# Attention into a mixture of experts on one core: rows written straight into their expert's list

## The chip, the cores and the metric

One core of a Trainium2 chip runs the whole program. The metric is device microseconds per execution; lower is better. Besides the times there is one profiled execution, whose trace gives the start and duration of every instruction and DMA, and who released whom.

## The reference

There are four batches of 3648 tokens with 256 channels. Attention runs over channels: q and k are normalized along the tokens, the 256 x 256 scores of a batch are summed over its tokens, and x = v @ softmax(scores). Then each token of x goes to one of 16 experts (4 groups of 4), and its result is weighted by two softmax values:

```python
qn = q / (np.linalg.norm(q, axis=1, keepdims=True) + 1e-06)
kn = k / (np.linalg.norm(k, axis=1, keepdims=True) + 1e-06)
a = softmax(kn.transpose(0, 2, 1) @ qn / tau)         # 4 x 256 x 256
x = (v @ a).reshape(14592, 256)
g = argmax(x @ w_group); e = argmax(x @ w_expert[g])  # one expert a token
h = np.maximum(x[tok] @ w1[g, e], 0.0)                # 256 -> 1024
out[tok] = (g_w * e_w)[:, None] * (h @ w2[g, e])      # 1024 -> 256
```

All is float32. The kernel gets near that by splitting each operand into a high and a low part and multiplying three times (high x high, high x low, low x high).

## The kernel before

**Scores.** 32 steps load a tile of q and k each (GPB = 8 tiles a batch: seven of 4 columns of 128 tokens, and a short one), split it and multiply. When a batch's scores are complete, a softmax follows.

**The x stage** runs 10 steps later, one tile u of v a step: SP loads it (`x_load`, line 264, tile `vr`), PE transposes it (`x_tr`, line 276, `vtr`), PE multiplies (`x_mm`, line 294, `xmm`), and ACT copies the result (line 297) into one of three buffers `xs`: 256 words of x and 20 router logits a token. ACT then issues the DMA that writes x to a DRAM table in token order (`x_scratch`, line 304).

**Routing.** `routing(b, j0, j1)` runs on DVE over a range of a batch's columns. It finds each token's expert, its place in that expert's list (`si`) and its weight, kept as pairs (token, weight) in `pr`. RANGES says how batches are cut. `scatter` issues on POOL one indirect DMA a column (line 387): 128 pairs of 8 bytes, to the places `si` of a table `slot_list` in DRAM. After each indirect DMA POOL fills a dummy tile (`pause`, line 125). 116 columns make 116 scatters; the first 78 (`PRE`: batches 0 and 1 and 20 columns of batch 2) are enough for the first four items.

**Items.** The expert work is 28 items of up to 512 tokens of one expert (and some small pieces, `q`, of 4 x 32). `tables_pre` picks items 0 to 3 from the counts over PRE; `tables_rest` picks the others once every token has a place. For an item, SP loads the list (`fetch_ids`, line 513, `slt`) and the expert's two weight matrices (`fetch_w`, line 508, three buffers `wraw`, 1 MB each); POOL gathers the rows (`fetch_x`, four gathers of 128 rows, line 519, `xg`); PE transposes, ACT and DVE split the rows (`xth`, `xtl`, lines 569 and 570) and the weights (`wh` on ACT, line 544; `wl` on DVE, line 545). An item has 8 steps f: `ffn1` (line 670, `hmm`), relu and split (`hh` on ACT, line 674; `hl` on DVE, line 675), and two steps later `ffn2` (line 686, `yacc`). At the end `put` weights the rows and scatters them to the output on POOL (line 696).

**Order.** SP and POOL run in written order; SP's queue holds loads of v, of lists and of weights alike, and an entry that waits holds up those behind it. In the expert stage a scheduler orders PE, ACT and DVE; their order is then fixed. ACT splits item i+1's weights between the `hh` of item i.

Of the kernel before, what the change touches and what calls it, by code (L numbers as in the profile page):

```python
# [11 lines left out]
I32 = mybir.dt.int32  # L12
# [17 lines left out]
NE = C + NL  # L30
BIG = 512
# [11 lines left out]
RANGES = [[(0, 16), (16, NJ)], [(0, 16), (16, NJ)], [(0, 16), (16, 20), (20, NJ)], [(0, NJ)]]  # L43
# [3 lines left out]
LOADS = 3  # L47
SPLIT = 3
# [6 lines left out]
def attention_moe(ctx: ExitStack, tc, q, k, v, tau, w_group, w_expert, w1, w2, out):  # L55
# [6 lines left out]
    xd = nc.dram_tensor("x_scratch", (N, C), F32, kind="Internal").ap()  # L62
    sl = nc.dram_tensor("slot_list", (NSLOT, 2), I32, kind="Internal").ap()
# [6 lines left out]
    ps = ctx.enter_context(tc.tile_pool(name="ps", bufs=2, space=PSUM))  # L70

# [35 lines left out]
    prs = {}  # L107
    for b in range(B):
        for j0, j1 in RANGES[b]:
            prs[b, j0] = t = cp.tile([P, j1 - j0, 2], I32, name=f"pr{b}_{j0}")  # L110
            n = min(j1, J) - j0
            POOL.iota(t[:, :n, 0], pattern=[[1, n]], base=b * NT + j0, channel_multiplier=J)
            if j1 == NJ:
                POOL.iota(t[:, n:n + 1, 0], pattern=[[0, 1]], base=b * NT + J * P, channel_multiplier=1)
    xgs = []
    for i in range(3):
        t = cp.tile([P, 4, C], F32, name=f"xg{i}")
        POOL.memset(t, 0.0)
        xgs.append(t)

    pad = cp.tile([P, 256], F32, name="pad")
# [8 lines left out]
    def fill_slots():  # L130
        n = NSLOT // P
        slz = spool.tile([P, n // 2, 2], I32, tag="slz", name="slz", bufs=1)
        POOL.memset(slz[:, :, 0:1], NOID)
        POOL.memset(slz[:, :, 1:2], 0)
        for h in range(2):
            SP.dma_start(sl[h * NSLOT // 2:(h + 1) * NSLOT // 2, :].rearrange("(p n) w -> p n w", p=P), slz)
# [144 lines left out]
    def x_mm(u, mid=None):  # L281
# [6 lines left out]
        xs = tp.tile([P, GJ, NE], F32, tag="xs", name="xs", bufs=3)  # L288
# [19 lines left out]
    scatters, pend, now = [], [], [0]  # L308
# [4 lines left out]
    def routing(b, j0=0, j1=NJ):  # L313
        nj = j1 - j0
        L = st[b]["L"][:, j0:j1, :]
        pr = prs[b, j0]

        def wide(nm, n, *shape):
            return rp.tile([P, NJ * n], F32, name=nm)[:, 0:nj * n]
# [48 lines left out]
        si = rp.tile([P, NJ], I32, name="si", bufs=4)[:, 0:nj]  # L368
# [27 lines left out]
    def table(items, cnt, start, stride, name):  # L396

        inc = rp.tile([1, E], F32, tag="tinc", name="tinc")
        DVE.tensor_tensor_scan(inc, onesf[0:1, 0:E], cnt, 0.0, ALU.mult, ALU.add)
        ge = rp.tile([1, items, E], F32, tag="tge", name="tge")  # L400
        ii = iof[0:1, 0:items]
        ib = lambda a: a.unsqueeze(2).broadcast_to([1, items, E])
        eb = lambda a: a.unsqueeze(1).broadcast_to([1, items, E])
        DVE.tensor_tensor(ge, ib(ii), eb(inc), ALU.is_ge)
        ex = rp.tile([1, items], F32, tag="tex", name="tex")
        DVE.tensor_reduce(ex, ge, AX.X, ALU.add)
        DVE.tensor_tensor(ge, ge, eb(inc), ALU.mult)
# [9 lines left out]
        nv = rp.tile([1, items], F32, tag="tnv", name="tnv")  # L417
        DVE.tensor_scalar(nv, ex, float(E), None, ALU.is_lt)
        DVE.tensor_scalar(st_, st_, float(-DUMMY), None, ALU.add)
        DVE.tensor_tensor(st_, st_, nv, ALU.mult)  # L420
        tb = rp.tile([1, items, 2], I32, name="tb_" + name)
        DVE.tensor_scalar(tb[:, :, 0], ex, float(E - 1), None, ALU.min)
        DVE.tensor_scalar(tb[:, :, 1], st_, float(DUMMY), None, ALU.add)
        return tb

    r16 = lambda nm: rp.tile([1, E], F32, name=nm)

    def shifted(x, sh, nm):
        i_ = rp.tile([1, E], I32, tag="shi", name="shi")
# [8 lines left out]
    def tables_pre():  # L438
        cnt = carry[0:1, :]
# [619 lines left out]
```

## Time and profile before

| | |
|---|---|
| median of 3 runs | 1002.72 us (1001.12 to 1002.72) |
| the profiled execution's own time | 1002.05 us |
| its span, first to last instruction | 1000.3 us |
| mean granted TensorE clock | 0.982 |
| busy: PE, DVE, POOL, ACT | 945.1, 563.2, 515.3, 474.0 us |
| moved by DMA | 202.17 MB |

The span lies 1.75 us below the profiled time, and that lies 0.67 us below the median. PE is busy for 94% of the span, so the first question is where its other 55 us lie and what it waited for there. PEclk is the share of TensorE's full clock that was granted in a stretch. An instruction marked SPq is the issue of a DMA by SP, not its transfer. In a timeline the brackets give the engine's idle time ahead of an instruction and what ended it.

### The profile page before, as it was taken

Reading aid. Unit: us, or ns where it says so; the run is one execution under the profiler, and the core shown is the slowest. Engines: PE = TensorE matmul, PEld = TensorE weight load, DVE = VectorE, ACT = ScalarE, POOL = GpSimd, SP = SyncE. Lnnn points to the kernel's source line nnn. Section 1 sums busy time; section 2 is a strip of 40 time slices with the busy share of each in tenths; the row PEclk is TensorE's granted clock in tenths of the full one; section 3 lists DMA queues with packets and bytes.
Section 4 is the critical chain, followed back from the end, with each engine's and each line's share of the span. In section 5 each row is a group of like instructions: output and inputs, shape, how many; then the busy total and the mean of one; then the engine's idle time right before and its main releaser. Section 6 shows DMA issues by size and latency. Waiting matters only on the chain.

```text
span 1000.3 us, 18385 instructions
## 1 busy us (share of the span) xinstructions
PE 945.1 (94%) x6428; PEld 831.4 (83%) x6428; DVE 563.2 (56%) x961; ACT 474.0 (47%) x763; POOL 515.3 (52%) x729
## 2 busy tenths in 40 slices
PE   7999999978899399999999999999999999999995
PEld 6899989867789298888888888888888888888885
DVE  6988988774798154444444444454445444544421
ACT  6777767445644134443444444444444444444421
POOL 2001989885868854445444544455444544454322
PEclk9999999989999799999999999999999999999998
DMA  8898788358720546666666666556655665565520
GB/s 300 322 373 271 243 253 264 110 179 272 233 86 1 180 140 211 212 211 216 212 211 208 210 218 206 198 202 215 201 201 203 209 209 194 198 223 198 195 74 25
DMA packets 125685, 202.17 MB, mean 202 GB/s; under 512 B 18946, under 2 KB 87562, under 8 KB 125584
## 3 DMA queue, kind: packets, MB, share of 16 engines
q1 hardware_dynamic: 93952, 155.92, 47.0%
q0 software_dynamic: 15040, 30.03, 8.5%
q10 hardware_dynamic: 16592, 14.97, 4.5%
q8 instruction: 52, 0.85, 0.4%
q14 instruction: 49, 0.40, 0.1%
HBM read 169.49 MB, written 32.43 MB: 202 GB/s over the span
## 4 chain that ended last, share of the span: by engine, by line
PE 37%; POOL 19%; issue 18%; DMA 1%; POOLq 1%; SPq 0%; DVE 0%; DVEq 0%
PE yacc L686 17%; PE hmm L670 16%; POOL xg L519 5%; POOL out L696 5%; POOL pad L125 4%; POOL slot_list L387 4%; PE qmm L780 1%; PE xtr L568 1%; PE qacc L797 1%; DMA wraw<-in_moe_w 1%; DMA slot_list<-pr,si 0%; PE qtr L787 0%; POOLq L519 0%; POOL qxg L749 0%; POOLq L696 0%
## 5 line engine op out<-in xcount | busy, mean ns | idle before, releaser
L696 POOL DMA_INDIRECT out<-ys,slt x112 | 129.4, 1155 | 328.3 <-ACT ys L693 312.4
L675 DVE SCALAR_TENSOR_TENSOR hl<-hmm,hh 128x512 fp32r<-128x512 f32 x224 | 154.1, 688 | 231.1 <-ACT hh L674 199.7
L686 PE MATMUL yacc<-wh,hh 128*128 128x256 f32 x896 | 254.3, 284 | 16.6 <-ACT hh L674 16.3
L674 ACT ACTIVATE hh<-hmm 128x512 fp32r<-128x512 f32 x224 | 132.9, 594 | 280.2 <-PE hmm L670 254.4
L686 PE MATMUL yacc<-wh,hl 128*128 128x256 f32 x896 | 250.6, 280 | 1.1 <-DVE hl L675 0.6
L686 PE MATMUL yacc<-wl,hh 128*128 128x256 f32 x896 | 250.4, 279 | 0.0
L545 DVE TENSOR_TENSOR wl<-wraw,wh 128x1024 fp32r<-128x1024 f32 x112 | 136.3, 1220 | 122.9 <-ACT wh L544 76.9
L686 PEld LDWEIGHTS yacc<-wh,hh 128*128 128x128 f32 x896 | 168.6, 188 | 39.7 <-ACT hh L674 24.2
L387 POOL DMA_INDIRECT slot_list<-pr,si x116 | 136.0, 1173 | 116.5 <-DVE vtl L278 89.1
L670 PE MATMUL hmm<-xth,wh 128*128 128x512 f32 x448 | 180.2, 402 | 1.9 <-ACT xth L569 1.9
L670 PE MATMUL hmm<-xtl,wh 128*128 128x512 f32 x448 | 177.7, 397 | 1.0 <-DVE xtl L570 1.0
L670 PE MATMUL hmm<-xth,wl 128*128 128x512 f32 x448 | 177.4, 396 | 0.0
L686 PEld LDWEIGHTS yacc<-wl,hh 128*128 128x128 f32 x896 | 168.6, 188 | 7.9
L686 PEld LDWEIGHTS yacc<-wh,hl 128*128 128x128 f32 x896 | 168.7, 188 | 1.4 <-DVE hl L675 0.9
L544 ACT ACTIVATE wh<-wraw 128x1024 fp32r<-128x1024 f32 x112 | 117.8, 1054 | 108.0 <-DMA wraw<-in_moe_w 78.1
L519 POOL DMA_INDIRECT xg<-x_scratch,slt x112 | 116.0, 1035 | 30.5 <-issue 28.0
L125 POOL MEMSET pad<- 128x256 f32 x352 | 117.4, 334 | 0.3
L670 PEld LDWEIGHTS hmm<-xth,wl 128*128 128x128 f32 x448 | 84.9, 189 | 19.5
L670 PEld LDWEIGHTS hmm<-xth,wh 128*128 128x128 f32 x448 | 84.9, 190 | 13.1 <-POOL pad L125 2.1
L670 PEld LDWEIGHTS hmm<-xtl,wh 128*128 128x128 f32 x448 | 84.9, 189 | 11.6 <-DVE xtl L570 1.3
L199 PE MATMUL sacc<-qkraw 128*128 128x256 f32 (+1 forms) x352 | 87.7, 391 | 5.7 <-DMA qkraw<-in_k 5.7
L199 PEld LDWEIGHTS sacc<-qkraw 128*128 128x128 f32 (+1 forms) x352 | 64.8, 195 | 14.1 <-DMA qkraw<-in_q 5.7
(184 smaller groups left out, 1232.4 us busy)
## 6 DMA issues: line engine op xcount, KB each, us to landing
wraw<-in_moe_w SPq DMA_DIRECT2D x56, 1024.0 KB
wraw<-in_moe_w SPq DMA_DIRECT2D x96, 512.0 KB
vr<-in_v SPq DMA_DIRECT2D x28, 512.0 KB
x_scratch<-xs ACTq DMA_DIRECT2D x28, 512.0 KB
qkraw<-in_q SPq DMA_DIRECT2D x27, 512.0 KB
qkraw<-in_k SPq DMA_DIRECT2D x27, 512.0 KB
slot_list<-slz SPq DMA_DIRECT2D x2, 930.0 KB
slot_list<-pr,si POOLq DMA_INDIRECT x116
```

Source lines behind the costliest of these rows:

```text
L125: POOL.memset(pad, 0.0)
L199: PE.matmul(d["acc"][:, c, :], kt[:rows, 1, cs], qt[:rows, 0, :], start=d.pop("first", True) and c == 0, stop=(g == NG), skip_group_check= ...
L387: ins = POOL.indirect_dma_start(out=sl, out_offset=bass.IndirectOffsetOnAxis(ap=si[:rows, j:j + 1], axis=0), in_=pr[:rows, j, :], in_offse ...
L519: POOL.indirect_dma_start(out=xg[:, t, :], out_offset=None, in_=xd[0:n, :], in_offset=bass.IndirectOffsetOnAxis(ap=d["sl"][:, t, 0:1], axi ...
L544: ACT.activation(whs[n][:, s], raw[:, s], AF.Copy)
L545: DVE.tensor_tensor(wls[n][:, s], raw[:, s], whs[n][:, s], ALU.subtract)
L568: PE.transpose(tr[:, t * P:(t + 1) * P], d["xg"][:, t, c * P:(c + 1) * P], ident)
L670: PE.matmul(mm, wt[:, c, fs], xt[:, c, :], start=(n == 0), stop=(n == 5))
L674: ACT.activation(hh, mm, AF.Relu)
L675: DVE.scalar_tensor_tensor(hl, mm, 0.0, hh, ALU.max, ALU.subtract)
L686: PE.matmul(a, ht[:, tsl], wt[:, f, :], start=(f == 0 and t % 2 == 0 and n == 0), stop=(f == 7 and n == 2), skip_group_check=True)
L696: ins = POOL.indirect_dma_start(out=out, out_offset=bass.IndirectOffsetOnAxis(ap=d["sl"][:, t, 0:1], axis=0), in_=ys[:, t, :], in_offset=N ...
```

## The change

`x_scratch`, `slot_list`, `fill_slots`, `fetch_ids` and the pairs `pr` go. A new DRAM table `x_sorted` has a row of RW = 272 words (1088 bytes) for every place in the lists: 256 words of x, the token's number and its weight. `routing` writes the weight into the `xs` buffer behind x, POOL writes the token numbers (an iota a tile), and `scatter` sends 128 whole rows of `xs` (139,264 bytes) where it sent 128 pairs. The write of x in token order is gone. `xs`, `xg` and `ys` share one ring of 10 buffers, so a buffer of `xs` is held until its rows have been scattered.

Items 0 to 3 are read by one plain SP DMA each; the first stands right behind the weights of item 0. Items from 4 on are read by one gather of 128 x 4352 bytes, from an index table `ix` that DVE makes, without an id load on SP. Places beyond the end of a list hold whatever was there, so 48 rows of zeros are scattered behind the lists' ends, and `tokens` (three small DVE operations an item, ordered behind the last subtraction of `split_x`) masks the token numbers there. The tables are computed on all 128 partitions, with some operations more. Batch 3 is routed in two ranges. The fill after gathers and output scatters is gone.

```diff
-RANGES = [[(0, 16), (16, NJ)], [(0, 16), (16, NJ)], [(0, 16), (16, 20), (20, NJ)], [(0, NJ)]]
+RANGES = [[(0, 16), (16, NJ)], [(0, 16), (16, NJ)], [(0, 16), (16, 20), (20, NJ)], [(0, 16), (16, NJ)]]
+RW = 272
+RING = 10
...
-        xs = tp.tile([P, GJ, NE], F32, tag="xs", name="xs", bufs=3)
+        xs = ring(GJ, NE, name="xs")
...
-        ACT.dma_start(xo, xs[:rows, :nj, :C])
...
-        DVE.reciprocal(pr[:, :, 1].bitcast(F32), se)
+        for g in range(j0 // GJ, -(-j1 // GJ)):
+            n = min(GJ, j1 - g * GJ)
+            DVE.reciprocal(rows_at[b, g][:, 0:n, C + 1], se[:, g * GJ - j0:g * GJ - j0 + n])
...
+            if t == 0:
+                tok = xs[:, 0:nj, C].bitcast(I32)
+                if g < NG:
+                    POOL.iota(tok, pattern=[[-1, GJ]], base=NOID - b * NT - g * GJ, channel_multiplier=-J)
...
             ins = POOL.indirect_dma_start(
-                out=sl, out_offset=bass.IndirectOffsetOnAxis(ap=si[:rows, j:j + 1], axis=0),
-                in_=pr[:rows, j, :], in_offset=None, bounds_check=NSLOT - 1, oob_is_err=False)
+                out=xs_d, out_offset=bass.IndirectOffsetOnAxis(ap=si[:rows, j:j + 1], axis=0),
+                in_=xs[:rows, t, 0:RW].bitcast(I32), in_offset=None, bounds_check=NSLOT - 1, oob_is_err=False)
...
+    def gather(rows, ix, per):
+        src = xs_d.rearrange("(n t) w -> n (t w)", t=per)
+        POOL.indirect_dma_start(out=rows.bitcast(I32), out_offset=None, in_=src,
+                                in_offset=bass.IndirectOffsetOnAxis(ap=ix, axis=0),
+                                bounds_check=NSLOT // per - 1, oob_is_err=False)
+
+    def tokens(ids, row, slot, nv, behind=None):
+        keep = hp.tile(list(slot.shape), I32, tag=f"keep{slot.shape[1]}", name="keep", bufs=2)
+        DVE.tensor_scalar(keep, slot, nv, -1.0, ALU.is_lt, ALU.mult)
+        ins = DVE.tensor_tensor(ids, row.bitcast(I32), keep, ALU.bitwise_and)
...
+        DVE.tensor_scalar(ids, ids, -1.0, float(NOID), ALU.mult, ALU.add)
...
-    def fetch_x(d, xg, n):
-        for t in range(4):
-            POOL.indirect_dma_start(out=xg[:, t, :], out_offset=None, in_=xd[0:n, :],
...
-            pause()
+    def fetch_x(d, tb, i):
+        d["xg"] = ring(4, RW, name="xg")
+        d["nv"] = tb[1][:, i:i + 1]
+        if tb is not tb_pre:
+            gather(d["xg"].rearrange("p t w -> p (t w)"), tb[2][:, i:i + 1], 4)
+            return
+        s = SP.value_load(tb[0][0:1, i, 1:2], min_val=0, max_val=DUMMY)
+        ins = SP.dma_start(d["xg"].bitcast(I32), xs_d[ds(s, BIG), :].rearrange("(p t) w -> p t w", t=4))
...
             fetch_w(items[0], tb_pre, 0, "w2")
-        if x == UX - 5:
-            for i in range(KPRE):
-                fetch_ids(items[i], tb_pre, i)
+            fetch_x(items[0], tb_pre, 0)
         if x == UX - 4:
-            fetch_x(items[0], xgs[0], N - NT)
+            fetch_x(items[1], tb_pre, 1)
...
-        scatter(8 if t + 2 >= US else 5, 0 if t + 2 >= US else 2, before)
+        scatter(8 if t + 2 >= US else 5, 0 if t + 2 >= US else 1)
...
-        if i >= KPRE:
-            fetch_ids(d, tb, k)
+        if i < KPRE:
+            fetch_x(d, tb, k)
         if weights:
             fetch_big(i, "w1")
             fetch_big(i, "w2")
-        if i >= 4:
-            fetch_x(d, xgs[i % 3], N if i >= KPRE else N - NT)
+        if i >= KPRE:
+            fetch_x(d, tb, k)
```

The first place where this moves instructions is SP's queue between the weights of item 3 and those of item 4 (the numbers are buffer numbers; `tb_pre` and `tb_big` are the tables of items 0 to 3 and of the others). Before:

```order
L508 ISA
L508 DMA wraw_3876<-in_moe_w2 128x8x256
L511 TENSOR_LOAD tb_big_4154
L511 ISA x2
L513 ISA
L513 DMA slt_4236<-slot_list 128x8
L505 TENSOR_LOAD tb_big_4154
L505 ISA x2
L508 ISA
L508 DMA wraw_4247<-in_moe_w1 128x2x1024
```

After:

```order
L590 DMA wraw_3873<-in_moe_w1 128x2x1024
L587 TENSOR_LOAD tb_pre_2677
L587 ISA x2
L590 ISA
L590 DMA wraw_3884<-in_moe_w2 128x8x256
L587 TENSOR_LOAD tb_big_4171
L587 ISA x2
L590 ISA
L590 DMA wraw_4304<-in_moe_w1 128x2x1024
```

The list load of item 4 (`slt_4236`) no longer stands between item 3's second weights (`wraw_3876`, now `wraw_3884`) and item 4's first (`wraw_4247`, now `wraw_4304`). The loads of the rows of items 2 and 3 now stand ahead of those items' weights.

The second place is SP's queue at the weights of item 0, where the last tiles of v (`vr`) are loaded too. Before:

```order
L508 DMA wraw_2918<-in_moe_w1 128x2x1024
L505 TENSOR_LOAD tb_pre_2666
L505 ISA x2
L508 ISA
L508 DMA wraw_2929<-in_moe_w2 128x8x256
L264 DMA vr_2985<-in_v 128x1024
L511 TENSOR_LOAD tb_pre_2666
L511 ISA x2
L513 ISA
L513 DMA slt_3012<-slot_list 128x8
```

After:

```order
L590 DMA wraw_2929<-in_moe_w1 128x2x1024
L587 TENSOR_LOAD tb_pre_2677
L587 ISA x2
L590 ISA
L590 DMA wraw_2940<-in_moe_w2 128x8x256
L599 TENSOR_LOAD tb_pre_2677
L599 ISA x2
L600 ISA
L600 DMA xg_2942<-x_sorted 128x1088
L271 DMA vr_3042<-in_v 128x1024
L271 DMA vr_3099<-in_v 128x1024
```

The load of tile 29 of v (`vr_2985`, now `vr_3042`) stood ahead of the first list load; it now stands behind the load of item 0's rows (`xg_2942`), which reads what the 78 scatters of PRE have written. Tile 30's (`vr_3099`) follows it directly.

## Rows read from the trace of the kernel before

**Rows 1.** Windows: stretch, us, busy PE, PEld, DVE, ACT, POOL; PEclk, DMA share, GB/s.

```profile
331.30:347.60 16.30, 0.01 (x1) 0.01 (x1) 0.52 (x1) 1.61 (x3) 14.39 (x23) 0.63 0.71 228
347.60:353.50 5.90, 5.32 (x20) 4.59 (x21) 4.77 (x6) 2.80 (x4) 3.48 (x4) 0.57 0.59 193
400.00:960.00 560.00, 559.50 (x3907) 481.13 (x3906) 267.60 (x357) 240.32 (x376) 260.71 (x364) 1.00 0.60 206
```

**Rows 2.** Waits of PE, 225 to 360 us: total us, times, longest.

```profile
PE yacc L686 <- ACT hh L674: 16.3, 1, 16.3
PE vtr L276 <- DMA vr<-in_v: 3.3, 1, 3.3
```

**Rows 3.** Timeline, 330 to 349 us: start, us, engine, instruction, idle before and releaser.

```profile
331.40 0.91 POOL L387 DMA_INDIRECT slot_list<-pr,si  x1 [0.17 <-issue]
334.40 0.34 SPq L513 DMA_DIRECT2D slt<-slot_list  x1
335.59 1.58 SPq L508 DMA_DIRECT2D wraw<-in_moe_w  x2
345.99 1.06 ACT L544 ACTIVATE wh<-wraw 128x1024 fp32r<-128x1024 f32 x1 [22.45 <-DMA wraw<-in_moe_w]
```

**Rows 4.** Chain of waits, 325 to 352 us: start, us, what.

```profile
331.40 2.75 DMA slot_list<-pr,si
```

**Rows 5.** Timeline of DVE, 299 to 310 us.

```profile
300.25 0.17 DVE L423 TENSOR_SCALAR tb_big<-tst 1x24 int32<-1x24 f32 x1
306.19 1.21 DVE L545 TENSOR_TENSOR wl<-wraw,wh 128x1024 fp32r<-128x1024 f32 x1
```

**Rows 6.** Timeline of POOL, two scatters.

```profile
227.48 0.97 POOL L387 DMA_INDIRECT slot_list<-pr,si  x1 [0.17 <-issue]
284.25 1.70 POOL L387 DMA_INDIRECT slot_list<-pr,si  x1 [5.91 <-DVE si L369]
```

**Rows 7.** All scatters of one line: ns min/median/max, first and last start.

```profile
L387 POOL DMA_INDIRECT slot_list<-pr,si x116: 913/972/3042, 96.2 to 331.4; - x116
```

**Rows 8.** Groups of POOL by form: busy us, mean ns of one, idle before.

```profile
L112 POOL IOTA pr<- 128x16 int32 x3 | 0.4, 132 | 0.0
L696 POOL DMA_INDIRECT out<-ys,slt x112 | 129.4, 1155 | 328.3 <-ACT ys L693 312.4 <-issue 15.6 <-DVE xtl L570 0.2
```

**Rows 9.** Timeline of SP, 195 to 315 us.

```profile
220.87 1.77 SPq L508 DMA_DIRECT2D wraw<-in_moe_w  x2
227.49 0.35 SPq L264 DMA_DIRECT2D vr<-in_v  x1
236.04 4.57 SPq L513 DMA_DIRECT2D slt<-slot_list  x4
240.63 1.46 SPq L264 DMA_DIRECT2D vr<-in_v  x2
```

**Rows 10.** Timeline of PE, 237 to 262 us.

```profile
238.29 1.03 PE L276 MATMUL vtr<-ident,vr 128*128 128x128 f32 x8
245.66 1.06 PE L276 MATMUL vtr<-ident,vr 128*128 128x128 f32 x8 [3.27 <-DMA vr<-in_v]
```

**Rows 11.** Windows of two earlier stretches, columns as in rows 1.

```profile
229.00:262.00 33.00, 26.45 (x184) 24.90 (x185) 15.75 (x39) 18.86 (x42) 20.21 (x29) 0.93 0.85 257
280.00:320.00 40.00, 40.00 (x263) 36.35 (x262) 39.66 (x112) 18.38 (x28) 30.65 (x41) 1.00 0.18 54
```

**Rows 12.** Timeline of ACT at item 4's tokens.

```profile
358.17 1.09 ACT L569 ACTIVATE xth<-xtr 128x512 fp32r<-128x512 f32 x2 [1.25 <-PE xtr L568]
```

**Rows 13.** The page's third part: queue, packets, MB, share of 16 engines.

```profile
q0 software_dynamic: 15040, 30.03, 8.5%
q10 hardware_dynamic: 16592, 14.97, 4.5%
```

**Rows 14.** Timeline of POOL at the end.

```profile
987.79 0.97 POOL L696 DMA_INDIRECT out<-ys,slt  x1 [13.08 <-ACT ys L693]
992.18 0.97 POOL L696 DMA_INDIRECT out<-ys,slt  x1 [0.16 <-issue]
```

More of the change, by code (lines that the diff above doesn't have):

```diff
@@ L106, in attention_moe @@
     DVE.memset(carry, 0.0)
[L107 to L119, printed above, removed]
+    slot4 = cp.tile([P, 4], F32, name="slot4")
+    slot1 = cp.tile([P, 1], F32, name="slot1")
+    slotq = cp.tile([P, 1], F32, name="slotq")
+    for t, m in ((slot4, 4), (slot1, 1)):
+        i_ = cp.tile(list(t.shape), I32, name=f"si{m}")
+        POOL.iota(i_, pattern=[[1, t.shape[1]]], base=0, channel_multiplier=m)
+        DVE.tensor_copy(t, i_)
+    for n in range(4):
+        DVE.tensor_scalar(slotq[n * PC:(n + 1) * PC, :], slot1[n * PC:(n + 1) * PC, :], float(-n * PC), None, ALU.add)
+    own = cp.tile([P, E], F32, name="own")
+    POOL.affine_select(own, onesf[:, 0:E], pattern=[[-3, E]], compare_op=ALU.is_ge, fill=0.0,
+                       base=0, channel_multiplier=1)
+    POOL.affine_select(own, own, pattern=[[3, E]], compare_op=ALU.is_ge, fill=0.0,
+                       base=2, channel_multiplier=-1)
+    part = cp.tile([P, 1], F32, name="part")
+    i_ = cp.tile([P, E], F32, name="own3")
+    DVE.scalar_tensor_tensor(i_, own, -3.0, iof[:, 0:E], ALU.mult, ALU.mult)
+    DVE.tensor_reduce(part, i_, AX.X, ALU.add)
+    DVE.tensor_tensor(part, part, slot1, ALU.add)
+    zero = cp.tile([P, RW], F32, name="zero")
+    DVE.memset(zero, 0.0)
     pad = cp.tile([P, 256], F32, name="pad")
@@ L125, in pause @@
         POOL.memset(pad, 0.0)
+    vp_ = ctx.enter_context(ExitStack())
+    vp = vp_.enter_context(tc.tile_pool(name="vp", bufs=3, side="right"))
     sp_ = ctx.enter_context(ExitStack())
     spool = sp_.enter_context(tc.tile_pool(name="spool", bufs=2))
[L130 to L136, printed above, removed]
     st = [dict() for _ in range(B)]
@@ new lines, in gather @@
+    def gather(rows, ix, per):
[7 more added lines that the diff above has]
+        ins = DVE.tensor_tensor(ids, row.bitcast(I32), keep, ALU.bitwise_and)
+        if behind is not None:
+            tc.add_manual_dep(ins.ins, behind.ins.name,
+                              mybir.DependencyInfo(mybir.DependencyClass.NoSync, mybir.DependencyReason.DATA),
+                              reason="the rows are there by then")
+        DVE.tensor_scalar(ids, ids, -1.0, float(NOID), ALU.mult, ALU.add)
@@ L473, in tables_rest @@
         s0 = r16("s0")
-        DVE.scalar_tensor_tensor(s0, used, float(BIG), ecap[0:1, :], ALU.mult, ALU.add)
-        tb = table(NREST, nb, s0, BIG, "big")
+        DVE.scalar_tensor_tensor(s0, used, float(BIG), ecap, ALU.mult, ALU.add)
+        held = r16("held2")
+        DVE.scalar_tensor_tensor(held, used, float(-BIG), cnt, ALU.mult, ALU.add)
+        tb = table(NREST, nb, s0, held, BIG, "big")
+        ixb = index(tb[2], tb[1], slot4[:, 0:1], 4, slot1, "big")
+        end = rp.tile([P, E], F32, name="end")
+        DVE.tensor_tensor(end, cnt, ecap, ALU.add)
+        DVE.tensor_tensor(end, end, own, ALU.mult)
+        ends = rp.tile([P, 1], F32, name="ends")
+        DVE.tensor_reduce(ends, end, AX.X, ALU.add)
+        endi = rp.tile([P, 1], I32, name="endi")
+        DVE.tensor_scalar(endi, ends, part, None, ALU.add)
+        ins = POOL.indirect_dma_start(
+                                out=xs_d, out_offset=bass.IndirectOffsetOnAxis(ap=endi[:3 * E, :], axis=0),
+                                in_=zero[:3 * E, :].bitcast(I32), in_offset=None, bounds_check=NSLOT - 1, oob_is_err=False)
+        for o in scatters:
+            tc.declare_no_dep(ins.ins, o, reason="these slots have no token")
         s1 = r16("s1")
-        DVE.scalar_tensor_tensor(s1, f, float(BIG), ecap[0:1, :], ALU.mult, ALU.add)
+        DVE.scalar_tensor_tensor(s1, f, float(BIG), ecap, ALU.mult, ALU.add)
         up = r16("up")
@@ L528, in attention_moe @@
     rgens = []
-    before = lambda r: r < PRE
     def advance(n):
@@ L621, in attention_moe @@
                 advance(1)
-            scatter(N, 0, before)
+            scatter(N)
             wp = ctx.enter_context(tc.tile_pool(name="wp", bufs=4))
@@ L658, in attention_moe @@
             sp_.close()
-    for i in range(1, 4):
-        fetch_x(items[i], xgs[i % 3], N - NT)
+    vp_.close()
     yscat = []
@@ L701, in put @@
         yscat.append(ins.ins)
-        pause()
     def finish(d):
-        d["ys"] = tp.tile([P, 4, C], F32, tag="xs", name="ys", bufs=3)
+        d["ys"] = ring(4, C, name="ys")
         for t in range(4):
@@ L962, in attention_moe @@
             d = items[NBIG - 1]
-            d["ys"] = tp.tile([P, 4, C], F32, tag="xs", name="ys", bufs=3)
+            d["ys"] = ring(4, C, name="ys")
             for t in (0, 2, 1, 3):
```

251 lines of the change are left out of this document (135 added, 116 removed).

## The prediction

> **What bounds the kernel now.** The windows come first. From 400 to 960 us PE is busy for 559.5 of 560 us at a granted clock of 1.00 [rows 1]. The change leaves PE's matrix work as it is, so nothing can be won there; what it can win or lose lies in the x stage, in the first items and at the end. The waits of PE name two places [rows 2]: one stall of 16.3 us ahead of `yacc` on ACT's `hh`, and 3.3 us ahead of `vtr` on a load of v.
>
> The timeline tells what stands behind the stall [rows 3]. ACT runs in a fixed order, and a split of item 4's first weights stands ahead of the `hh` that PE wants. ACT waited 22.45 us for those weights, until 345.99 us. SP issued them only at 335.59, behind the load of item 4's list at 334.40, and that had waited for the last scatter into `slot_list`, which POOL began at 331.40 and which landed 2.75 us later [rows 4]. Yet the choice of items was ready at 300.25, and the last split that held the buffer of item 4's second weights began at 306.19 and took 1.21 us [rows 5]. So SP stood some 27 us behind a list that nobody needed yet. After the stall PE ran at less than full speed: the granted clock was 0.57 from 347.6 to 353.5 us, a mixture of its two levels (1.2 and 2.4 GHz), after 16.3 us in which PE did nothing [rows 1]. In clock alone that is 5.9 x (1 - 0.57) = 2.5 us.
>
> **The change part by part.** The sum is made against the profiled execution, 1002.05 us, which lies 0.67 us below the median of 1002.72.
>
> *Item 4's weights.* The list load between item 3's weights and item 4's goes. The first of them then needs the item choice (300.25) and a buffer that is free by then, the second the buffer of the split at 306.19 [rows 5]. From issue to use such loads took 345.99 - 335.59 = 10.4 us [rows 3]: issued at 300.5 and 307.5, they are there at 311 and 318, and ACT came to the first at 345.99 - 22.45 = 323.5. If all of it moves by the 4 us that the x stage may lose below, ACT's need moves along. The stall goes with its slow clock: -16.3 - 2.5 = **-18.8 us**. What could be late next are item 4's rows: they now need the zero rows, which follow all scatters and the outputs of two items on POOL. In the trace of before the last 29 scatters started at 284.25 [rows 6], since the routing of batch 3 was done then. Now 16 of them go earlier and the 13 of the second range start there, or some us later: 13 x 1.46 + 4 x 0.30 (below) = 20.2, to 304.5; eight outputs at 1.14 to 1.16 [rows 8, 14] make 314 (the second item's have to wait for their results, which puts 318 as a late end); the zero rows 1.16 + 2.75, the gather 1.16 + 2.75: 322 to 326. ACT split item 4's rows at 358.17 [rows 12], 339 without the stall. 13 us cover it.
>
> *Weight and token in the row, and POOL's pace.* The scatters of PRE ran from 96.2 [rows 7] to the last one's start at 227.48 [rows 6], 77 steps of 1.70 us; a quiet step is 1.46 (the end's, [rows 14]: (992.18 - 987.79) / 3). The price on POOL of a scatter of 1024-byte rows is that of 8-byte rows: 1155 against a median of 972 ns, in both kinds with a minimum below 1 us for the smaller [rows 7, 8], so the range is 0 to +0.18 a scatter and I take 0: POOL makes as many descriptors, only longer ones. An iota costs 132 ns [rows 8] and some 0.17 us ahead of it [rows 6], 0.30 in all. PRE has 21 tiles: +6.3 us, and the last PRE scatter starts at 233.8.
>
> *DMA.* The write of x went 14.97 MB in 16592 packets for 4.5% of 16 engines, 0.30% a MB; POOL's queue took 8.5% for 30.03 MB, 0.28% a MB [rows 13]. The new scatters move 116 x 139,264 bytes = 16.2 MB, so 4.6% replace 4.5%: nothing. ACT loses 32 DMA issues. No row here has PE waiting for them: 0.
>
> *The v loads behind item 0's rows.* SP's load of item 0's rows waits until the PRE scatters have landed, and tile 29 of v is queued behind it (order above). A landing took 2.75 us in a quiet stretch [rows 4]; at PRE's end it was at most 236.04 - 227.48 = 8.56, with 2 MB of weights under way since 220.87 [rows 6, 9]. So the rows are issued at 236.6 to 242.4 and tile 29 up to 1.1 us later (four list loads took 4.57). From issue to use a load of v took 245.66 - 240.63 = 5.0 us [rows 9, 10]: it is there at 242 to 248.5. PE transposed it at 238.29 [rows 10] (its load had been issued at 227.49). PE waits 4 to 10 us, but the 3.27 that it waited for tile 30 go, which now comes with tile 29. Net +0.7 to +6.9; I take **+2.0**, near the quiet landing, since the weights of 220.87 are over by then. If the landing hid altogether, -3.3.
>
> The Trainium skill's page "DMA: Bandwidth & Descriptors", section "Anatomy of one DMA — SWDGE (gpsimd) path", fits a POOL DMA by 2.0 us + bytes / 436e3; for 139,264 bytes that makes an estimate of 2.3 us. By it tile 29 would cost about +0.3 here, and the sum would be 1.7 lower. The quiet 2.75 us agrees roughly, the 8.56 does not.
>
> *The ring.* In the x stage the tiles follow each other by 4.1 us here (245.66 - 3.27 - 238.29, [rows 10]). Tile 29 gets the buffer of batch 2's sixth tile, the first whose scatters all come after PRE's, and tile 30 that of the seventh. Those cost 4 x 1.46 + 0.30 = 6.1 us a tile, so the sixth is out at 241 and landed at 244 to 249, the seventh at 250 to 255. With the wait for v, tiles 29 and 30 are written from about 243 and 248 on. ACT can wait 1 to 7 us; the three PSUM buffers of `xmm`, three columns of some 1 us each, cover about 3 for PE: I take **+1.0**, range 0 to 4.
>
> *DVE.* From 280 to 320 us it is busy 39.66 of 40 while PE never waits [rows 11]. Three tables get five operations more each, and index tables, list ends and masks come on top, some 30 in all. If all cost what the last of `tb_big` took (0.17, [rows 5]) that is 5 us; some are wider, and I estimate 5 to 10. Half of batch 3's routing leaves this stretch. Most of the new work has no one waiting for it; if a tenth to a fifth gets ahead of an `hl`, **+1.0**, range 0 to 4.
>
> *The end.* The last four outputs stood 1.46 us apart, 0.97 each, the fill between them; without it 1.14. The last begins 3 x 0.32 = **-1.0 us** earlier [rows 14].
>
> Sum: -18.8 + 2.0 + 1.0 + 1.0 - 1.0 = -15.8. 1002.05 - 15.8 = 986.2 us, and with 0.67 for the median **987.0 us**. Its own range: 982 to 993, from the ends of the terms.
>
> **Rivals.** *All covers hold.* The landing is quick, the ring never waits, DVE hides its work: -18.8 - 1.0 - 3.3 = -23.1, 979.6 us. For it: PE is idle for 6.5 of 33 us from 229 to 262 [rows 11], of which only the waits named are explained, so slack is there. Against it: the order on SP puts a landing ahead of tile 29, which has no such wait now.
>
> *Part of the stall stays.* The rows of items 2 and 3 now stand ahead of their weights on SP and wait for ring buffers that scatters of batch 3 set free, or item 4's gather is late. PE stopped at 331.3, 7.8 us after ACT had come to the weights; each us by which they come after that costs one. Between no stall and all of it I take half: -9.4 instead of -18.8, 996.4 us. For it: SP's queue is written so. Against: 16 of batch 3's columns are out before 284.
>
> *POOL becomes the bound: slower.* If long rows raise the step of a PRE scatter, each 0.1 us delays item 0's rows, tile 29 and all behind it by 78 x 0.1 = 7.8 us. The gain of 15.8 is used up when the step goes from 1.70 to 1.90; at 2.0 the time is 987.0 + 23.4 = 1010.4 us. The ring of 10 then backs up too. For it: single scatters took up to 3042 ns [rows 7], and the stretch is full of DMA (0.85, [rows 11]). Against: POOL's outputs of 1024-byte rows keep to 1155 ns [rows 8], and in both programs a scatter waits for the one 8 before it, 13.6 us at the present step, against a landing of at most 8.56.
>
> The Trainium skill's page "DMA: Bandwidth & Descriptors", section "How a descriptor splits into AXI transactions", speaks for this rival: a descriptor that does not start on 256 bytes pays for its first partial piece. By its counting rows of 1088 bytes, three in four of which start off such a boundary, take 34 to 40 beats where 1024 take 32. By that the estimate of 4.6% becomes 5.7% of the engines at most, a quarter more time on each row. No row of before has such rows.
>
> *The change doesn't do what it says:* something else holds SP until the last scatter, and the stall stays whole: 1002.05 + 3.0 + 0.7 = 1005.7 us.
>
> **How the numbers follow.** Forecast 0.55, all covers 0.14, part of the stall 0.16, POOL 0.11, no effect 0.04. A measurement of this kernel tells about 0.2%, 2 us, from no change. Below 1000.7 lie the first three: faster 0.84, with 0.01 taken off for their upper ends; within 2 us of 1002.72, by the tails of three cases, 0.04; slower 0.12. The range from 979 to 1003 us leaves out the slow cases and little of the first.
>
> **What would show it.** Right: no wait of PE above 3 us after 262 us; the clock at 1.00 there; SP's first weights of item 4 issued between 297 and 312; the last PRE scatter near 234, `vtr` waiting 4 to 6 us once near 240; the outputs at the end 1.14 apart. Wrong: scatters of over 1.9 us a step, `xmm` waiting for `xs` by many us before 229, a wait of ACT for `wraw` or of PE for `xg` after 310, or `hl` late between 280 and 330.

## The result and the profile after

| | before | after |
|---|---|---|
| median, us (4 runs each, same chip) | 1001.92 (999.32 to 1002.72) | 991.87 (990.29 to 992.75) |
| profiled execution: time, span, us | 1002.05, 1000.3 | 992.31, 990.6 |
| busy PE, DVE, POOL, us | 945.1, 563.2, 515.3 | 951.2, 590.8, 356.0 |

The ratio is 0.9902, interval 0.9879 to 0.9926: about 10 us faster, where 15.8 were forecast. The direction was right and the time lies inside both ranges, but some 6 us of the gain are missing (the median is 4.9 us above the forecast, the span fell by 9.7). First the waits of PE after, from 225 to 360 us (total us, times, longest):

```profile
PE vtr L283 <- DMA vr<-in_v: 4.4, 1, 4.4
PE yacc L766 <- DVE ys L775: 3.1, 2, 1.7
PE hmm L750 <- DVE xtl L653: 2.4, 1, 2.4
PE hmm L750 <- ACT xth L652: 1.2, 1, 1.2
```

The 16.3 us ahead of `yacc` are gone [rows 2]. The wait for v is there as foreseen, and there is a small new one: `yacc` on DVE's `ys`. The windows (columns as in rows 1):

```profile
260.00:267.00 7.00, 6.38 (x16) 5.07 (x17) 5.45 (x12) 3.40 (x5) 6.23 (x10) 0.52 0.22 80
280.00:300.00 20.00, 18.60 (x123) 16.78 (x122) 18.04 (x55) 9.62 (x15) 17.80 (x27) 1.00 0.73 238
300.00:320.00 20.00, 18.25 (x119) 16.44 (x119) 19.50 (x77) 8.49 (x13) 12.18 (x16) 1.00 0.29 104
340.00:360.00 20.00, 20.00 (x131) 18.14 (x130) 10.63 (x17) 8.51 (x14) 6.85 (x6) 1.00 0.46 160
400.00:960.00 560.00, 560.00 (x3889) 481.72 (x3891) 273.55 (x427) 237.31 (x371) 139.84 (x116) 1.00 0.57 201
```

From 340 to 360 us, where PE stood and then ran at 0.57 [rows 1], it is busy all the time at 1.00. But from 280 to 320 PE is busy for 36.85 of 40 us, where it was busy for all 40 [rows 11]; near 260 there are 7 us at 0.52; and from 400 to 960 PE, busy throughout at 1.00, has 3889 matmuls where it had 3907. A busy engine can be slower: look at its count too.

Where the span's 9.7 us come from is seen at the first `hmm` of each item. For item 4, before and then after (timeline of PE):

```profile
372.44 0.40 PE L670 MATMUL hmm<-xth,wh 128*128 128x512 f32 x1
```

```profile
358.20 0.39 PE L750 MATMUL hmm<-xth,wh 128*128 128x512 f32 x1
```

| first `hmm` of item | 0 | 1 | 2 | 3 | 4 | 11 | 20 | 27 | last `yacc` ends |
|---|---|---|---|---|---|---|---|---|---|
| before, us | 258.34 | 283.24 | 306.52 | 329.75 | 372.44 | 552.70 | 782.45 | 961.71 | 989.26 |
| after minus before | -0.6 | +0.9 | +2.7 | +5.0 | -14.2 | -13.7 | -11.5 | -10.0 | -9.7 |

So four pieces: the x stage -0.6; from the first `hmm` of item 0 to that of item 3, 5.6 us are lost; the stall gives back 19.2; and then, with no wait in sight, each item loses about 0.2 us, 4.5 in all. The end itself gives 0.

On SP (timeline), item 4's weights are no longer behind a list:

```profile
234.95 0.35 SPq L600 DMA_DIRECT2D xg<-x_sorted  x1
235.40 0.86 SPq L271 DMA_DIRECT2D vr<-in_v  x2
...
282.63 44.02 SPq L590 DMA_DIRECT2D wraw<-in_moe_w  x4
```

The four loads of the last row are item 3's two and item 4's two, issued at 282.63, 288.46, 297.32 and 326.28. So item 4's second weights were still late: SP waited 27.6 us for a split on DVE (`wl`) that set their buffer free, and ACT waited 2.20 us for them, without a wait of PE (waits of SP, 280 to 335 us; timeline of ACT):

```profile
SPq L590 <- DVE wl L625: 27.6, 1, 27.6
```

```profile
333.47 2.01 ACT L624 ACTIVATE wh<-wraw 128x1024 fp32r<-128x1024 f32 x2 [2.20 <-DMA wraw<-in_moe_w]
```

On POOL (timeline) stand the last scatter of PRE, the last of all, the zero rows and the gather of item 4; then, in the kernel before, the first of item 4's four gathers:

```profile
230.86 0.97 POOL L404 DMA_INDIRECT x_sorted<-xs,si  x1 [0.17 <-DVE vtl L285]
...
305.91 0.94 POOL L404 DMA_INDIRECT x_sorted<-xs,si  x1 [1.95 <-issue]
...
321.70 1.27 POOL L545 DMA_INDIRECT x_sorted<-zero,endi  x1 [0.30 <-issue]
324.58 1.06 POOL L467 DMA_INDIRECT xg<-x_sorted,ix_big  x1 [1.61 <-DMA x_sorted<-zero,endi]
```

```profile
344.50 1.05 POOL L519 DMA_INDIRECT xg<-x_scratch,slt  x1 [0.16 <-issue]
```

The last scatter starts at 305.91 instead of 331.40 [rows 3], and the gather of item 4, which stands behind it on POOL, at 324.58 instead of 344.50. The experiments show that the gain hangs on this.

The scatters by their line (ns min/median/max, first and last start; then landing), and the queues of the page's third part:

```profile
L404 POOL DMA_INDIRECT x_sorted<-xs,si x116: 927/982/3097, 86.4 to 305.9; - x116
...
DMA to landing us min/median/max: 2.3/4.4/8.2
```

```profile
q0 software_dynamic: 14944, 44.54, 11.8%
q10 hardware_dynamic: 1488, 0.02, 0.1%
```

A scatter of 1088-byte rows costs POOL 982 ns at the median, one of 8-byte rows 972 [rows 7]. The two queues together take 11.9% of the engines, where they took 13.0% [rows 13].

### The profile page after: what moved, and what is told of

Its sections match the earlier page's. It is cut to its first block, busy times and chain, and to the rows that moved or that the text cites. A ratio compares the mean times of both kernels' runs of the same rounds, so it can differ in the third digit from the quotient of the medians.

```text
span 990.6 us, 17747 instructions
## 1 busy us (share of the span) xinstructions
PE 951.2 (96%) x6430; PEld 836.6 (84%) x6430; DVE 590.8 (60%) x1159; ACT 475.0 (48%) x764; POOL 356.0 (36%) x425
## 4 chain that ended last, share of the span: by engine, by line
PE 67%; DVE 5%; issue 3%; POOL 2%; DMA 2%; ACT 0%; SPq 0%; POOLq 0%; DVEq 0%; ACTq 0%
PE yacc L766 29%; PE hmm L750 28%; PE qacc L870 2%; PE qmm L853 2%; PE xtr L651 2%; PE xmm L302 2%; POOL x_sorted L404 1%; DVE wl L625 1%; DMA wraw<-in_moe_w 1%; DVE hl L755 1%; PE qtr L860 1%; DMA vr<-in_v 1%; PE vtr L283 0%; POOL pad L138 0%; POOL out L776 0%
## 5 line engine op out<-in xcount | busy, mean ns | idle before, releaser
L776 POOL DMA_INDIRECT out<-ys,ids x112 | 136.0, 1215 | 486.7 <-ACT ys L773 458.8
L404 POOL DMA_INDIRECT x_sorted<-xs,si x116 | 137.2, 1183 | 62.3 <-issue 36.3
L302 PE MATMUL xmm<-ahi,vth 128*128 128x276 f32 (+1 forms) x232 | 71.2, 308 | 2.8 <-ACT xs L305 2.0
L302 PE MATMUL xmm<-alo,vth 128*128 128x276 f32 (+1 forms) x232 | 69.4, 300 | 0.4 <-DVE alo L263 0.4
```

The source lines that it names most:

```text
L302: PE.matmul(mm[:rows, :NE], vt[:, c, j * P:j * P + rows], at[:, c, :], start=(n == 0), stop=(n == 5))
L404: ins = POOL.indirect_dma_start(out=xs_d, out_offset=bass.IndirectOffsetOnAxis(ap=si[:rows, j:j + 1], axis=0), in_=xs[:rows, t, 0:RW].bitc ...
L776: ins = POOL.indirect_dma_start(out=out, out_offset=bass.IndirectOffsetOnAxis(ap=d["ids"][:, t:t + 1], axis=0), in_=ys[:, t, :], in_offset ...
```

## The experiments

All kernels were timed beside the kernel before on the same chip; the ratio is to that, and of the changed kernel it is 0.9902. Letters in the expectations: A, SP's order held item 4's weights back and alone made the stall; B, all of item 4, its rows too, was late because POOL ended its scatters late; C, the addresses of the tiles in SBUF set PE's pace; E, the rows of items 2 and 3 ahead of their weights on SP make DVE late; F, DVE's new tables do; I and J, two rules on addresses.

**Order or POOL's end?** b_swap: in the kernel before, the list load goes behind item 4's weights:

```diff
-        if i >= KPRE:
-            fetch_ids(d, tb, k)
         if weights:
...
+        if i >= KPRE:
+            fetch_ids(d, tb, k)
```

> The kernel before with one edit: from item 4 on SP loads an item's two weight matrices ahead of its list. Theory A (the list load on SP alone made the stall, nothing is late next): the 16.3 us wait of PE and its slow clock go, 1002 - 19 = 983 us. Theory B (in the kernel before all of item 4 was late, the rows too, because POOL's scatters ended at 332 and eight outputs and the gathers follow them): the weights come at about 310 and 318, but item 4's gathers still start at about 344.5 and land near 352, while PE wants the rows at 339; PE waits some 10 to 13 us there and the time is 992 to 998 us.

Measured: 1003.50 us, ratio 1.0010 (0.9993 to 1.0027). SP's timeline, then the waits of PE:

```profile
298.67 12.15 SPq L508 DMA_DIRECT2D wraw<-in_moe_w  x2
335.12 1.54 SPq L513 DMA_DIRECT2D slt<-slot_list  x2
```

```profile
PE xtr L568 <- DMA xg<-x_scratch,slt: 16.0, 4, 13.3
```

The weights are issued 37 us earlier than in rows 3, and PE waits as long for item 4's rows. Their gathers stand on POOL behind all scatters and eight outputs, and start right behind these:

```profile
345.99 1.05 POOL L519 DMA_INDIRECT xg<-x_scratch,slt  x1 [0.16 <-issue]
```

A falls: the order alone is worth nothing. B's own price, 10 to 13 us of waiting, was too low.

a_look, the other way round: in the changed kernel a small load that waits for all scatters goes ahead of item 4's weights:

```diff
+        if i == KPRE:
+            at = SP.value_load(tb_pre[0][0:1, 0, 1:2], min_val=0, max_val=DUMMY)
+            ins = SP.dma_start(pad[0:16, 0:2].bitcast(I32), xs_d[ds(at, 16), 0:2])
...
```

> The changed kernel, with one small load put back ahead of item 4's weights on SP: it reads 16 x 2 words of the sorted table and waits, as the list load did, until all 116 scatters have landed. Theory A (the place of that wait on SP is what cost 16 us): the stall comes back for the most part, 1000 us or more. Theory B (the scatters now end at 307 instead of 332, and that alone makes the wait harmless): item 4's first weights are issued at about 311 instead of 297, ACT wants them at 333, no wait of PE, 992 us, within 2 us of the changed kernel.

Measured: 994.52 us, 0.9924 (0.9899 to 0.9949). SP's timeline:

```profile
309.21 0.24 SPq L805 DMA_DIRECT2D pad<-x_sorted  x1
310.69 14.81 SPq L592 DMA_DIRECT2D wraw<-in_moe_w  x2
```

SP waits for the scatters as before, but they have landed by 309, and PE has no stall. The bad order does no harm once POOL is done early.

a_pool: POOL is to be made late again in the changed kernel, by 70 more fills (`pause`), written ahead of the scatters of batch 3's second range:

```diff
+                    for _ in range(70):
+                        pause()
```

> The changed kernel, with 70 fills of the dummy tile (0.334 us each, 23.4 us) put on POOL ahead of the scatters of batch 3's second range, so that the scatters end at about 330 as in the kernel before; SP's order stays as changed. Theory B (the stall went because POOL is done 25 us earlier): the zero rows and item 4's gather come 23 us later, the gather at about 348, landed near 355, while PE wants the rows at about 342; PE waits 10 to 14 us there, 1003 to 1008 us. Theory A (the stall went because item 4's weights no longer stand behind a list on SP): 992 us, at most 2 more.

Measured: 1001.32 us, 1.0016 (1.0000 to 1.0031). Waits of PE, and on POOL the last scatter, the fills and the gather of item 4:

```profile
PE xtr L651 <- DMA xg<-x_sorted,ix_big: 7.4, 1, 7.4
```

```profile
305.52 1.33 POOL L404 DMA_INDIRECT x_sorted<-xs,si  x1 [1.95 <-issue]
...
320.98 25.86 POOL L138 MEMSET pad<- 128x256 f32 x70
...
349.99 1.06 POOL L467 DMA_INDIRECT xg<-x_sorted,ix_big  x1 [1.60 <-DMA x_sorted<-zero,endi]
```

The fills ran elsewhere than was expected: the scatters end as in the changed kernel (305.52), and the fills stand behind them and behind the outputs of two items. So what this run makes late is the zero rows and item 4's gather, and nothing ahead of them. With the gather 25.4 us later the whole gain is gone; the wait is 7.4 us (10 to 14 expected), and half clock follows from 351.4 to 358.3 us. Late rows of item 4 alone cost the gain, with its weights issued as in the changed kernel.

Taken together: in the kernel before, item 4's weights and its rows were both late. With late rows the order on SP gives nothing (b_swap), and with POOL early the old wait on SP costs nothing (a_look). That the late scatters made the rows late there is read from POOL's timeline, where from 284.25 us to the last of those gathers no idle stretch is longer than 1.97 us; no run moves the scatters by themselves.

**The pace.** b_shift: in the kernel before, two unused tiles shift `hh`, `hl`, `wh` and `wl` to the addresses that they have in the changed kernel (`wh` and `wl` have four buffers each, and the fourth keeps its own; other tiles behind the gaps move too):

```diff
+    gap1 = cp.tile([P, 336], F32, name="gap1")
...
+        gap2 = hp.tile([P, 16], F32, name="gap2", bufs=1)
```

> The kernel before with two unused gaps in SBUF (1344 and 64 bytes a partition) that put hh, hl and wh0 to wh2, wl0 to wl2 at the addresses that they have in the changed kernel; no instruction changes. Theory C (the 2 ns that each yacc matmul is longer in the changed kernel come from where these tiles lie): yacc goes from 279 to 281 or 282 ns, an item takes about 0.2 us longer from item 5 on, 1002 + 5 = 1007 us. Theory D (they come from what else runs, or from DMA traffic): no change, 1002 us and yacc at 279 to 280.

Measured: 1008.20 us, 1.0058 (1.0036 to 1.0079). a_align: in the changed kernel the addresses of before, modulo 512 bytes, are put back (the dummy tile moves into the zero tile, and gaps are laid); in three more kernels other addresses are chosen in the same way:

```diff
-    pad = cp.tile([P, 256], F32, name="pad")
+    pad = zero[:, 0:256]
+    gap1 = cp.tile([P, 48], F32, name="gap1")
...
+            gap3 = wq.tile([P, 24], F32, name="gap3", bufs=1)
...
+        gap2 = hp.tile([P, 112], F32, name="gap2", bufs=1)
```

> The changed kernel with POOL's dummy tile laid into the tile of zeros and three unused gaps, so that hh, hl, wh and wl have the same remainders by 512 bytes as in the kernel before (64 and 384); the same instructions. Theory C (the addresses set the pace of yacc): yacc back to 279 or 280 ns, 992 - 4 = 988 us. If the remainder by 512 is not what counts, or by theory D: 992 us.

Measured: 986.64 us, 0.9838 (0.9810 to 0.9865). a_zero: all at a multiple of 512 (gaps of 32, 120, 32 words):

> The changed kernel laid out as in the aligned one, but with gaps that put hh, hl, wh and wl all on multiples of 512 bytes. If the distance between hh and wh by 512 bytes sets the pace (320 in the kernel before and in the aligned one, 384 and 96 in the changed one): at 0 another pace than 119.3 or 117.5 ns from yacc to yacc, faster or slower. If only a remainder other than a multiple of 64 (32 for wh3) or the like did harm: 117.5 ns and 987 us.

Measured: 994.78 us, 0.9951 (0.9932 to 0.9970). a_dist: `hh` at 384, `wh` at 192 (no gap1, then 72, 112):

> The changed kernel in a third layout: hh and hl at remainder 384 by 512 bytes as in the changed kernel, wh and wl at 192, so that their distance is 320 as in the kernel before and in the aligned one. Theory I (the distance of wh from hh by 512 sets the pace of yacc): 117.5 ns, 279 ns a matmul, 987 to 988 us. Theory J (the remainder of hh and hl counts, 64 being fast): 119 to 120 ns, 992 us.

Measured: 985.35 us, 0.9853 (0.9835 to 0.9871). a_hh64: `hh` at 64, `wh` at 256 (48, 56, 80):

> The changed kernel in a fourth layout: hh and hl at remainder 64 by 512 bytes as in the aligned one, wh and wl at 256 as in the changed one (distance 192). Theory I (the distance counts): 119 to 120 ns from yacc to yacc, 992 us. Theory J (the remainder of hh and hl counts): 117.5 ns, 987 to 988 us.

Measured: 986.98 us, 0.9863 (0.9847 to 0.9879).

The pace is read off ACT's timeline: the split of tokens (`xth`) of items 5 and 27, 22 items apart, here before, then after, then before with shifted tiles:

```profile
383.76 1.09 ACT L569 ACTIVATE xth<-xtr 128x512 fp32r<-128x512 f32 x2 [0.98 <-PE xtr L568]
...
947.50 1.08 ACT L569 ACTIVATE xth<-xtr 128x512 fp32r<-128x512 f32 x2 [1.42 <-PE xtr L568]
```

```profile
369.54 1.09 ACT L652 ACTIVATE xth<-xtr 128x512 fp32r<-128x512 f32 x2 [1.31 <-PE xtr L651]
...
937.38 1.09 ACT L652 ACTIVATE xth<-xtr 128x512 fp32r<-128x512 f32 x2 [1.59 <-PE xtr L651]
```

```profile
384.55 1.09 ACT L570 ACTIVATE xth<-xtr 128x512 fp32r<-128x512 f32 x2 [1.41 <-PE xtr L569]
...
952.76 1.09 ACT L570 ACTIVATE xth<-xtr 128x512 fp32r<-128x512 f32 x2 [1.74 <-PE xtr L569]
```

| kernel | `hh`, `hl` mod 512 | `wh`, `wl` mod 512 | `wh` - `hh` | first to last split, us | items 16 to 19, us |
|---|---|---|---|---|---|
| before | 64 | 384 | 320 | 563.74 | 102.25 |
| changed, addresses put back | 64 | 384 | 320 | 563.86 | 101.83 |
| changed, `hh` 384, `wh` 192 | 384 | 192 | 320 | 560.02 | 101.78 |
| changed, `hh` 64, `wh` 256 | 64 | 256 | 192 | 560.93 | 101.93 |
| changed | 384 | 256 (one 480) | 384 (96) | 567.84 | 103.19 |
| before, shifted | 384 | 256 (last as before) | 384 | 568.21 | 103.28 |
| changed, all 0 | 0 | 0 | 0 | 569.73 | 103.52 |

The last column goes from the first `hmm` of item 16 to that of item 20, four items in which PE has no break in any of these kernels. In the first two rows it stops now and then elsewhere: in the second, five times between the two splits, 2.1 us in all, and an item with such a break is up to 2.1 us longer than its like (waits of PE, 368 to 933 us):

```profile
PE yacc L768 <- issue: 1.7, 4, 0.8
PE hmm L752 <- DVE hl L757: 0.4, 1, 0.4
```

So the near equality of the first two rows over 22 items is chance. C stands in both directions: the shift alone costs the kernel before 1.0 us over four items, and putting the addresses back gives the changed kernel 1.4. The clock is 1.00 in all of them. D is weak: six kernels with the changed kernel's addresses but other edits (the changed kernel itself, a_look, a_pool, a_wfirst, a_late, a_vr) take 567.84 to 567.90 us over the 22 items. Yet the remainders are not all: with the same ones the kernel before takes 0.4 us longer over four items than the changed one. The groups of `yacc` and of one `hmm` (400 to 960 us: busy us, mean ns of one), for the changed kernel and then for `hh` 384, `wh` 192:

```profile
L766 PE MATMUL yacc<-wl,hh 128*128 128x256 f32 x696 | 195.8, 281 | 0.0
L750 PE MATMUL hmm<-xth,wl 128*128 128x512 f32 x349 | 137.9, 395 | 0.0
```

```profile
L767 PE MATMUL yacc<-wl,hh 128*128 128x256 f32 x708 | 197.2, 279 | 0.0
L751 PE MATMUL hmm<-xth,wl 128*128 128x512 f32 x353 | 137.5, 390 | 0.0
```

Counted from start to start, `yacc` goes from 120.7 to 118.8 ns and `hmm` from 235.3 to 232.0: with 96 and 48 of them an item, each makes about half of the 0.35 us.

Neither I nor J holds as written: distances of 320 and 192 are fast, 0 and 384 slow, and `hh` may be at 64 or 384. Five layouts don't make a rule; which property counts stays open. So does why the all-0 kernel's ratio stands 0.5% (5 us) above the changed kernel's, more than its pace explains; its profiled execution, 991.46 us, was among its fastest.

**Items 0 to 3.** a_wfirst: in the changed kernel the weights of items 2 and 3 go ahead of their rows on SP:

```diff
-        if i < KPRE:
-            fetch_x(d, tb, k)
         if weights:
...
-        if i >= KPRE:
-            fetch_x(d, tb, k)
+        fetch_x(d, tb, k)
```

> The changed kernel, with the weights of items 2 and 3 ahead of their rows on SP. Theory E (DVE is late around 293 and 317 because item 2's second weights wait on SP behind item 2's rows, and so for scatters of batch 3): they are issued at about 263 instead of 270, their split moves from 281.9 to about 277, the two waits of PE on ys (1.4 and 1.7 us) shrink to 1 us in sum, 990 us. Theory F (DVE simply has too much to do between 283 and 325): the waits stay, 992 us.

Measured: 987.87 us, 0.9883 (0.9859 to 0.9907). SP's timeline, and PE's waits:

```profile
259.06 0.37 SPq L590 DMA_DIRECT2D wraw<-in_moe_w  x1
263.34 0.37 SPq L590 DMA_DIRECT2D wraw<-in_moe_w  x1
269.08 0.34 SPq L600 DMA_DIRECT2D xg<-x_sorted  x1
```

```profile
PE yacc L766 <- DVE ys L775: 1.4, 1, 1.4
```

In the changed kernel item 2's weights were issued at 268.28 only, behind rows that waited for scatters, and the chain of waits (225 to 340 us) goes on from them:

```profile
268.28 0.37 SPq L590
...
270.02 10.68 DMA wraw<-in_moe_w
280.78 1.07 ACT wh L624
281.87 1.23 DVE wl L625
```

Issued at 259.06 and 263.34, half of the wait for `ys` goes, and item 2 starts 3.0 us earlier (306.23) and item 3 3.4 (331.34), of which item 0 was already 1.1 earlier. The profile speaks for E: in the four other kernels with these addresses and this order on SP (a_look, a_pool, a_late, a_vr) the wait is 2.6 to 4.1 us. It is one profile, though, and the ratios differ by 0.2%, which their intervals don't separate. The rival, a_late: the table of small pieces, which only the last items need, moves behind item 3's last `hl`:

```diff
+            tc.add_manual_dep(ins.ins, behind.ins.name, ...)
...
+            if (i, f) == (4, 1):
+                tb_sub, nsub = tables_sub(items[3]["hl"])
```

> The changed kernel, with the table of the blocks of 128 (some 25 operations on DVE, 8 us between 311 and 325, used only after the last item) ordered behind item 3's last relu split, near 341. Theory F (too much on DVE): the second wait on ys (1.7 us near 318) goes, the first (1.4 near 293) stays; 990 us. Theory E: both stay, 992 us.

Measured: 992.20 us, 0.9924 (0.9902 to 0.9945). Waits of PE:

```profile
PE yacc L769 <- DVE ys L778: 3.4, 2, 2.5
```

In sum the wait stays. But the second one, which F would have go, is 0.88 us instead of 1.75 (PE's timeline), and the first, which should have stayed, 2.54 instead of 1.40. F isn't supported, and not ruled out.

**The wait for v.** a_vr: the rows of item 0 go behind tiles 29 and 30 of v, those of item 1 behind tile 31:

```diff
+        if x == UX - 4:
             fetch_x(items[0], tb_pre, 0)
-        if x == UX - 4:
+        if x == UX - 3:
             fetch_x(items[1], tb_pre, 1)
```

> The changed kernel, with the loads of the rows of items 0 and 1 behind those of tiles 29 to 31 of v on SP. Theory G (the wait of 4.4 us for tile 29 is what the new order on SP costs, and nothing else holds the x stage): the wait goes, item 0's first hmm starts at 254 instead of 257.7, 988 us. Theory H (the ring of 10 is next: tiles 29 and 30 of x have to wait for scatters of batch 2 that leave POOL at 241 and 247): PE waits on xs instead, item 0 starts at 257, 991 to 992 us.

Measured: 993.00 us, 0.9939 (0.9915 to 0.9962). Waits of PE:

```profile
PE xmm L302 <- ACT xs L305: 2.6, 1, 2.6
PE yacc L767 <- DVE ys L776: 4.1, 2, 2.8
PE hmm L751 <- DVE xtl L653: 3.6, 1, 3.6
```

The wait for v is gone and item 0 starts 3.8 us earlier (253.88), but waits for the ring and for DVE take its place, and the median gains nothing.

**Both gains in one kernel.** Addresses `hh` 384, `wh` 192, and weights first:

> The changed kernel in the third layout (hh and hl at remainder 384, wh and wl at 192), and with the weights of items 2 and 3 ahead of their rows on SP. If the two gains add up: the layout's 1.5% against the kernel before, and some 0.2% of the order (1.7 to 3 us of waits on DVE), a ratio of 0.982 to 0.984, 982 to 984 us. If the waits on ys come back in the faster layout, where PE asks DVE earlier: 0.985 to 0.986.

Measured: 986.38 us, 0.9851 (0.9823 to 0.9878); a wait of 2.7 us for `ys` remains, and PE stops three times between items 5 and 27 of its profile, 1.3 us in all. The two gains don't add up to anything that can be measured over the addresses alone: the three kernels with faster addresses have 0.9838 to 0.9863, and these intervals overlap.

## Why the prediction was right or wrong

- **The stall, -18.8: the size right, the cause only half.** The piece measures -19.2. The step put it down to SP's order; b_swap shows that the order alone gives 0, and a_pool that late rows of item 4 alone cost the gain. The step had that in its second half, as a cover: item 4's rows there at 322 to 326 (the gather started at 324.58 and took 4.4 to land). In the kernel before, item 4's gathers stood at 344.50 to 349.68 on POOL's timeline, so its rows were as late as its weights. A cover that the change itself brings about is part of the gain. POOL ended earlier because 13 instead of 29 scatters were left at 284. It had time for the 16 others since it no longer has the 16 gathers of items 0 to 3, in which it spent 29.6 us from 229 to 335 (16.5 busy and 13.1 idle ahead of them), nor the 5.91 us of waiting for batch 3's routing [rows 6]; in their place it was idle once for 9.4 us, up to 257.93. No run parts the missing gathers from the second range of batch 3.
- **Item 4's second weights: 19 us later than forecast, and covered.** They were to be issued at 307.5; it was 326.28, behind a split on DVE, and the wait of ACT for `wraw` that the prediction named as a sign of being wrong came, with 2.20 us. PE didn't feel it. The split that frees the buffer is not the one at 306.19 [rows 5] but the next: in b_swap the load went at 310.45, when that one, begun at 309.22, was done.
- **POOL's pace and DMA, 0: right in the result, in part by luck.** The scatter keeps its duration, and the last PRE scatter started at 230.86, 3 us before the 233.8 forecast. But PRE took 144.5 us, not the 131.3 of before and 6.3 for the iotas: a step of 1.88 us, just under the 1.90 of the slower rival, with more idle time on POOL. What hid that is the first scatter, which started at 86.4 instead of 96.2; the prediction hadn't foreseen it.
- **By the Trainium skill**, "DMA: Bandwidth & Descriptors", section "How a descriptor splits into AXI transactions", a row that starts off a 256-byte boundary pays for a partial piece. The queues' share fell here from 13.0% to 11.9%, but with 16432 packets instead of 31632, so no run shows that price or its absence. (The estimate of 5.7% counts the longer rows twice; 4.6 x 40 / 34 is 5.4.) The estimate of 2.3 us for a landing, by that page's section "Anatomy of one DMA — SWDGE (gpsimd) path", agrees with the fastest of the 116 landings and not with the median of 4.4.
- **The v loads, +2.0: right.** PE waited 4.4 us once (4 to 10 forecast), 3.27 for tile 30 went: net +1.1. **The ring, +1.0: its cover held.** ACT waited 5.4 us for POOL's fills and 2.3 for a scatter's landing, PE hardly. Yet item 0 starts 0.6 us earlier, not 3 later: at tile 28 PE was already 2.2 us ahead (232.18 against 234.34), and in the 50 us before 230 it was busy for 45.8 instead of 40.1. I had not priced that, and no run isolates it.
- **DVE, +1.0: too small.** `ys` made PE wait 3.1 us, and from 280 to 320 PE lost 3.15. The step blamed DVE's new operations; a_late doesn't bear that out. The profile of a_wfirst speaks for SP's order: item 2's weights behind its rows, which the rival "part of the stall stays" had named and priced at 9.4. The 5.6 us from item 0 to item 3 add up roughly: from item 0's first `hmm` on PE waits 5.5 us (`ys` 3.1, `xtl` 2.4) where it waited 2.0; the clock from 260 to 267 us is 0.52 where it was 0.76, which is 7 x 0.24 = 1.7; and the slower pace below takes some 3 x 0.23 = 0.7.
- **The step that failed most: "the change leaves PE's matrix work as it is, so nothing can be won there".** The instructions are the same, but not the addresses of their tiles. This missing term is +4.5 us, most of the difference between 987.0 and 991.87. b_shift and a_align show it. That the rest came out so near is luck: against the forecast the x stage was 3.6 us better and items 0 to 3 were 4.6 us worse.
- **The end, -1.0: 0.** The last outputs start 1.27 us apart, not 1.14 (0.97 and a gap of 0.30, not 0.17), and the last starts 2.33 us after the last `yacc` instead of 2.92 [rows 14]; but the program then takes 0.6 us longer to its end. The last row of POOL's timeline:

```profile
981.89 0.97 POOL L776 DMA_INDIRECT out<-ys,ids  x1 [0.30 <-issue]
```

## What to carry to other kernels

When an instruction waits for a late producer, ask what else of the same item waits for that producer; moving one waiter ahead of it only makes the next one late, and the gain belongs to what makes the producer earlier. When a change adds or resizes buffers, compare the addresses of the tiles that the matrix engine reads, and compare the pace of a stretch that is busy in both kernels (the time between two fixed events), since no view of waits shows it. A plain reordering can be tried with one moved line before it is credited with a stall. And look in the trace where an experiment's inserted work ran before reading its time: the fills of a_pool stood behind what they were to delay.

## What the hardware showed beside that

The same matmuls of the changed kernel, with PE busy without a break at a granted clock of 1.00, take 560.0 to 569.7 us for 22 items when nothing but the layout in SBUF differs (and POOL's fills go to another tile). The difference of up to 1.7% lies in the step from matmul to matmul, of 128x256 (118.8 ns against 120.7 for `hh` 384, `wh` 192 against the changed kernel) and of 128x512 (232.0 against 235.3), not in a wait of any engine. Which tile's address does it, and by what rule, is not shown.
